# Six instead of four of a unit's 64 blocks of exponentials on VectorE and GpSimd

## The chip, the cores and the metric

The kernel runs on one core of one Trainium2 chip. The metric is device microseconds of that core for one execution, the median of several runs. TensorE multiplies matrices into PSUM, ScalarE (ACT) evaluates exp and tanh, VectorE (DVE) does elementwise work and moves results out of PSUM, GpSimd (POOL) does a little elementwise work, and SyncE (SP) issues most DMAs.

## The reference

```python
def _A_ref(x, wqkv, wo):                        # x 1 x 2048 x 512, H = 32 heads of Dh = 16
    qkv = ((x @ wqkv).reshape(B, S, 3, H, Dh)).transpose(2, 0, 3, 1, 4)
    q, k, v = qkv[0], qkv[1], qkv[2]
    scores = jnp.einsum("bhqd,bhkd->bhqk", q, k) * (Dh ** -0.5)
    p = softmax(scores, axis=-1)
    o = jnp.einsum("bhqk,bhkd->bhqd", p, v)
    return o.transpose(0, 2, 1, 3).reshape(B, S, D) @ wo

def _B_ref(x, w1, w2, w3, w4):
    h = gelu(layernorm(x) @ w1)
    # the four quarters of h's columns shifted by 1, -1, 2, -2 positions
    x1 = x + shifted(h) @ w2
    return x1 + gelu(layernorm(x1) @ w3) @ w4

g = sigmoid((x * gate_w).sum(-1, keepdims=True))
out = g * _A_ref(x, ...) + (1 - g) * _B_ref(x, ...)
```

Attention holds 32 x 2048 x 2048 exponentials. All else is small beside them for ScalarE.

## The kernel before

**Units and blocks.** The queries are cut into four chunks of 512 columns, the 32 heads into eight groups of four. A *unit* (c, u) is one chunk with one group of heads: 32 units. A unit has 16 key tiles of 128 (kt) times four heads (j) = 64 *blocks*. A block is 128 keys by 512 queries of one head: one score matmul with 32 rows of the array (`score`, L620), an exponential of 512 columns, and one matmul with v (`attend_block`, L720) that adds into the unit's accumulator `acc`. There is one accumulator bank (pool `psA`). Column 0 of v is one, so that row of `acc` is the softmax's denominator. At a unit's end `finish_unit` copies `acc` to SBUF (L755), sends the denominators through DRAM to spread them over partitions, and scales (L768, L774).

**Slots.** The program is written out by hand as a row of slots, not scheduled by a tool. In slot i the loop at the end emits ScalarE's exponential of slot i (`expo(i)`, L712: one instruction over two or three blocks), the scores of slot i + 2 (`scores(i + 2)`), the attends that have become ready (`attend_ready`), then work beside the attention (`beside`), filling matmuls with zeros (`fill`, L863), and the steps that have fallen due (`run_due`). The first 34 slots (`EARLY`, the young phase) hold two blocks each; later ones three, in three PSUM banks. Slots alternate between two sides of PSUM, so TensorE writes the scores of a slot while ScalarE reads the one before.

**Blocks that ScalarE doesn't get.** From the third unit on (`DUNIT = 2`) the four blocks of the last key tile (`DKT`, kt = 15) go another way. Four slots of a unit, 1, 4, 7 and 10 after its start (`DAT`), hold two blocks of the row for ScalarE, and the third bank (`dsc`) holds the scores of such a block. `whole` then computes the exponential as a product of a power of two and a cubic polynomial:

- VectorE evacuates the scores times a factor to a 32-bit integer y (L628): the high half is the whole part of the power of two, the low half its fraction.
- GpSimd makes two linear terms of the low half, `ec` (L643) and `ea` (L645), in f16.
- VectorE makes the power of two from the high half, `t0` (`power`, L651, once for each block), then for two blocks at once, 1024 columns: the square of `ec` (L654), plus one (L658), times `ea` (L662), and times the power (`product`, L667), read as bf16.

Two such blocks are a *pair*; two pairs may be open (`epool`, `state["pairs"]`). A finished pair is put in `products`, and `attend_whole` attends it once its unit has an accumulator.

**What sets the order.** `due(slots, rank, cost, fn)` puts a step off by so many slots. `run_due` runs what is due in order of rank, and passes over a step with a cost while the planner's clock says that VectorE is more than `HORIZON` = 1.9 us ahead of TensorE, for at most `OVER` = 4 slots. The clock (`clock`, `vec`, `tensor`, `evac`) is a sum of fixed costs kept while the program is written. `beside` gets a credit for each slot, `CREDIT` = 0.52 us of matmuls, times `DSHARE` = 0.55 in a slot with a block for VectorE, and spends it on projections, the MLP (`gelu_pair`, with tanh on ScalarE, L332, and scalar_tensor_tensor on VectorE, L336), and output tiles (`out_tile`, L446, L454). One matmul of these costs 0.225. `fill` pads TensorE to `FILL` = 2 matmuls a slot, `DFILL` = 1 in a slot with a block for VectorE. `hurry` forces all due steps when a pair's buffers or the accumulator are needed. The q tile of a group of heads is projected from the first slot of the unit before on (`urgent`).

Of the kernel before, what the change touches and what calls it, by code (L numbers as in the profile page):

```python
# [30 lines left out]
def kernel(  # L31
# [51 lines left out]
    otp = ctx.enter_context(tc.tile_pool(name="otp", bufs=2))  # L83
# [71 lines left out]
    state = {"slot": 0, "gen": 0, "young": True, "now": 0, "hurried": 0, "gelus": 0, "mm": 0, "idle": False}  # L155
    later = []
    asides = deque()
    DKT = (NT - 1,)
    DUNIT = 2
    FIRST, CHAIN, TAIL = 0, 1, 2  # L160
    SLACK = 0.3
# [144 lines left out]
    def gelu_pair(w, m, rhs, dst, key):  # L306

        yield from wait_for(lambda: state["gelus"] < 3)
        state["gelus"] += 1
        yh = gelp.tile([P, 2, CH], BF16, tag="yh", name="yh")  # L310
        sq = gelp.tile([P, 2, CH], BF16, tag="sq", name="sq")
        for r in range(2):
            ps = gen("ps_y")
            yield from proj(ps, w, slice((m + r) * P, (m + r + 1) * P), rhs, GELU)
            evac(0.69).tensor_scalar(out=yh[:, r, :], in0=ps[:], scalar1=0.5, scalar2=None, op0=ALU.mult)  # L315
            if r == 0:
                yield MM * GELU
# [12 lines left out]
        def tanh():  # L330
            clock["act"] += 0.97
            nc.scalar.activation(out=sq[:], in_=sq[:], func=ACT.Tanh)  # L332
            due(2, TAIL, 1.2, gate_up)

        def gate_up():
            vec(1.25).scalar_tensor_tensor(out=dst, in0=sq[:], scalar=1.0, in1=yh[:], op0=ALU.add, op1=ALU.mult)  # L336
# [208 lines left out]
    def run_due(all=False):  # L545

        now = state["slot"]
        for item in sorted((x for x in later if x[0] <= now), key=lambda x: (x[1], x[0], x[2])):
# [5 lines left out]
        if asides and now >= EARLY // 2 and max(clock["vector"], clock["act"]) + 0.7 < clock["pe"] + HORIZON:  # L554
# [9 lines left out]
    row, start, todo = [], {}, {}  # L564
    for n, (c, u) in enumerate(units):
        start[n] = len(row)
        todo[(c, u)] = NT if n < DUNIT else NT + len(DKT)
        row += [(c, u, kt, j) for kt in range(NT) if n < DUNIT or kt not in DKT for j in range(4)]

    DAT = (1, 4, 7, 10)  # L570
    slots, extra, i = [], {}, 0
    unit, wait = 0, []
    while i < len(row):
        if i >= start.get(unit + 1, len(row)):
            unit += 1
        if i >= start[unit] and wait is not None and unit >= DUNIT and unit not in extra:
            extra[unit] = True
            wait = [(len(slots) + d, kt, j) for kt in DKT for d, j in zip(DAT, range(4))]
            left = {kt: [0, 1, 2, 3] for kt in DKT}
        w = 2 if len(slots) < EARLY else 3  # L580
        bl = row[i:i + w]
        if wait and len(slots) >= wait[0][0] and i + 2 < len(row):
            kt = wait[0][1]
            free = [j for j in left[kt] if j not in {b[3] for b in row[i:i + 2]}]
            if free and row[i + 1][:2] == units[unit]:
                wait.pop(0)
                left[kt].remove(free[0])
                bl = row[i:i + 2]
                extra[(len(slots),)] = units[unit] + (kt, free[0])
        slots.append((i, bl))  # L590
        i += len(bl)
    assert not wait
    extra = {k[0]: v for k, v in extra.items() if isinstance(k, tuple)}
# [30 lines left out]
    def whole(dsc, c, u, kt, j):  # L624


        y = ypool.tile([P, CH], I32, tag="y", name="y")
        vec(0.69, clock["pe"] + 0.2).tensor_scalar(out=y[:], in0=dsc[:], scalar1=65536.0 * DH ** -0.5 / LN2,  # L628
                                scalar2=127.5 * 65536.0, op0=ALU.mult, op1=ALU.add)
        group = halves.setdefault((c, u, kt), [])  # L630
        r = len(group) % 2
        group.append(j)
        if r == 0:
            while state["pairs"] == 2:
                hurry()
            state["pairs"] += 1
            halves["now"] = [epool.tile([P, 2, CH], t, tag=tag, name=tag)
                             for tag, t in (("t0", I16), ("ea", F16), ("ec", F16))]
        t0, ea, ec = halves["now"]
        lo = y[:].bitcast(U16).rearrange("p (n k) -> p n k", k=2)[:, :, 0]  # L640
        hi = y[:].bitcast(I16).rearrange("p (n k) -> p n k", k=2)[:, :, 1]
        g = LN2 / 65536.0
        nc.gpsimd.tensor_scalar(out=ec[:, r, :], in0=lo, scalar1=g / IM, scalar2=(RE - LN2 / 2) / IM,  # L643
                                op0=ALU.mult, op1=ALU.add)
        nc.gpsimd.tensor_scalar(out=ea[:, r, :], in0=lo, scalar1=CUB * IM * IM * g,  # L645
                                scalar2=CUB * IM * IM * (REAL - LN2 / 2), op0=ALU.mult, op1=ALU.add)

        pair = group[-2:]

        def power():  # L650
            vec(0.44).tensor_scalar(out=t0[:, r, :], in0=hi, scalar1=0.0, scalar2=128.0, op0=ALU.max, op1=ALU.mult)  # L651
# [5 lines left out]
        def one():  # L657
            vec(0.5).tensor_scalar(out=ec[:], in0=ec[:], scalar1=1.0, scalar2=None, op0=ALU.add)  # L658
            due(1, CHAIN, 0.7, cubic)

        def cubic():
            vec(0.75).tensor_tensor(out=ec[:], in0=ec[:], in1=ea[:], op=ALU.mult)  # L662
            due(1, CHAIN, 0.7, product)

        def product():
            pe = t0[:].bitcast(BF16)
            vec(0.75).tensor_tensor(out=pe, in0=ec[:], in1=pe, op=ALU.mult)  # L667
# [56 lines left out]
    def attend(a):  # L724

        c, u, kt, _ = row[a]
# [106 lines left out]
    def attend_ready():  # L833
        while waiting:
            a = waiting[0]
# [3 lines left out]
            if kt == 0 and (accs or state["slot"] < freed["at"] + 2):  # L839
                if not accs or slot_of[a][0] > state["now"] - 3:  # L840
# [4 lines left out]
                continue  # L845
# [19 lines left out]
    for i in range(NS):  # L865
# [4 lines left out]
        while 4 * ready + 3 <= lo + len(bl) - 1:  # L870
            waiting.append(4 * ready)
# [40 lines left out]
```

## Time and profile before

| | |
|---|---|
| median of 3 runs | 954.34 us (952.54 to 955.73) |
| the profiled execution's own time | 954.31 us |
| its span, first to last instruction | 952.1 us |
| mean granted TensorE clock | 0.967 |
| PE busy | 831.2 us (87%) |
| ACT busy | 910.0 us (96%) |
| DVE busy | 625.7 us (66%) |
| POOL busy | 192.8 us (20%) |

Busy time is the union of an engine's instructions. Consecutive matmuls and consecutive activations overlap, so their mean durations don't add up to it. An idle time is put down to the instruction that ended it. In the groups, `out<-in` names tiles, then come the shapes, the count, and after the bar the busy time in us, the mean of one in ns, the idle time in front in us, and what ended it.

### The profile page before, as it was taken

To read this page: it belongs to the slowest core of one execution; us is meant where nothing else is said; L and a number is where in the kernel's file an instruction comes from. 1 tells how busy PE (TensorE), PEld (TensorE's weight loads), DVE (VectorE), ACT (ScalarE), POOL (GpSimd) and SP (SyncE) were. 2 spreads that over 40 slices of the span, in tenths; PEclk is the share of its full clock that TensorE was granted. 3 is DMA by queue.
4 is the path that set the end of the run, shared out by engine and by line. 5 is a ranking of instruction groups with operands and counts; after the bars stand their busy time and mean duration, and the time that the engine had idled before them with its cause. 6 is when DMAs were issued, how large, how long until landed. Compare 5 with 4: busy or idle time off the path is not lost.

```text
span 952.1 us, 14507 instructions
## 1 busy us (share of the span) xinstructions
PE 831.2 (87%) x5631; PEld 252.0 (26%) x5631; DVE 625.7 (66%) x1100; ACT 910.0 (96%) x735; POOL 192.8 (20%) x281
## 2 busy tenths in 40 slices
PE   8999888889988889988789888889888899888886
PEld 2222222222222222222222222222222222222221
DVE  3776788778777764768754877755777744344436
ACT  5889999999999999999999999999999999999994
POOL 3012122222211211212121213112112112222220
PEclk9997999999998999999999989999999999999998
DMA  9601000000000000000000000000000100000000
GB/s 213 191 12 56 1 13 12 12 13 13 1 12 13 12 12 10 26 12 12 13 13 5 9 12 23 24 9 5 12 13 13 34 12 3 12 12 12 13 12 23
DMA packets 30381, 22.28 MB, mean 23 GB/s; under 512 B 16744, under 2 KB 25832, under 8 KB 30312
## 3 DMA queue, kind: packets, MB, share of 16 engines
q1 hardware_dynamic: 28680, 20.17, 7.3%
q10 hardware_dynamic: 1632, 1.18, 0.5%
q8 instruction: 44, 0.72, 0.3%
q14 instruction: 25, 0.20, 0.1%
HBM read 17.17 MB, written 2.35 MB: 21 GB/s over the span
## 4 chain that ended last, share of the span: by engine, by line
ACT 58%; issue 23%; PE 15%; DMA 2%; DVE 2%; SPq 0%; DVEq 0%; ACTq 0%
ACT pt L712 55%; PE stage L620 5%; ACT sq L332 3%; PE acc L720 3%; PE ps_v L209 2%; DMA bcs<-rec_d 1%; PE acc L863 1%; PE ps_y L209 1%; PE ps_o L209 1%; PE ps L209 1%; PE ps_k L209 1%; DMA wq<-in_A_wqkv_dram 1%; PE ps_t L297 0%; PE ps_q L209 0%; DVE rr L792 0%
## 5 line engine op out<-in xcount | busy, mean ns | idle before, releaser
L712 ACT ACTIVATE pt<-stage 128x1536 bf16<-128x1536 f32 (+1 forms) x694 | 882.9, 1492 | 24.1 <-PE stage L620 19.4
L620 PE MATMUL stage<-qT,kT 32*128 32x512 bf16 x1928 | 277.6, 390 | 106.5 <-ACT pt L712 83.8
L643 POOL TENSOR_SCALAR ec<-y 128x512 f16<-128x512 uint16 x120 | 86.0, 717 | 643.0 <-DVE y L628 642.8
L620 PEld LDWEIGHTS <-kT 32*128 32x128 bf16 x2048 | 101.5, 91 | 373.6 <-issue 333.8
L720 PE MATMUL acc<-pt,vp 128*17 128x512 bf16 (+1 forms) x1928 | 194.7, 394 | 0.2
L863 PE MATMUL acc<-wq,zero 128*128 128x512 bf16 x480 | 165.7, 394 | 0.0
L628 DVE TENSOR_SCALAR y<-dsc 128x512 int32<-128x512 f32 x120 | 82.5, 687 | 119.3 <-PE dsc L620 118.8
L209 PE MATMUL ps_y<-xnT,w 128*128 128x512 bf16 x288 | 99.8, 395 | 2.0 <-DVE yh L315 1.4
L645 POOL TENSOR_SCALAR ea<-y 128x512 f16<-128x512 uint16 x120 | 89.0, 742 | 9.5
L315 DVE TENSOR_SCALAR yh<-ps_y 128x512 bf16<-128x512 f32 x72 | 49.6, 689 | 50.2 <-PE ps_y L209 49.7
L720 PEld LDWEIGHTS <-vp 128*17 128x17 bf16 (+1 forms) x2048 | 48.7, 88 | 117.1 <-issue 117.0
L209 PE MATMUL ps<-w,g2T 128*128 128x512 bf16 x224 | 65.9, 384 | 0.0
L651 DVE TENSOR_SCALAR t<-y 128x512 int16<-128x512 int16 x120 | 59.8, 499 | 0.3
L620 PE MATMUL dsc<-qT,kT 32*128 32x512 bf16 x120 | 48.1, 401 | 0.0
L863 PEld LDWEIGHTS <-zero 128*128 128x128 bf16 x480 | 35.6, 98 | 45.0 <-issue 44.8
L654 DVE TENSOR_TENSOR ec<-ec 128x1024 f16<-128x1024 f16 x60 | 41.0, 683 | 4.6 <-POOL ec L643 4.6
L332 ACT ACTIVATE sq<-sq 128x1024 bf16<-128x1024 bf16 x36 | 43.5, 1209 | 0.0
L667 DVE TENSOR_TENSOR t<-ec,t 128x1024 bf16<-128x1024 f16 x60 | 42.6, 710 | 1.3
L662 DVE TENSOR_TENSOR ec<-ec,ea 128x1024 f16<-128x1024 f16 x60 | 41.5, 692 | 2.3
L209 PEld LDWEIGHTS <-w 128*128 128x128 bf16 x288 | 22.8, 97 | 56.1 <-issue 54.2
L774 DVE TENSOR_TENSOR oT<-accsb,bcs 128x512 bf16<-128x512 f32 x31 | 22.4, 724 | 22.5 <-DMA bcs<-rec_d 22.5
L336 DVE SCALAR_TENSOR_TENSOR g2T<-sq,yh 128x1024 bf16<-128x1024 bf16 x28 | 35.3, 1260 | 0.3 <-ACT sq L332 0.3
(81 smaller groups left out, 539.2 us busy)
## 6 DMA issues: line engine op xcount, KB each, us to landing
bcs<-rec_d SPq DMA_DIRECT2D x31, 256.0 KB
w<-in_B_w_dram SPq DMA_DIRECT2D x2, 1792.0 KB
x_sb<-in_A_x_dram SPq DMA_DIRECT2D x14, 128.0 KB
out_dram<-ot SPq DMA_DIRECT2D x14, 128.0 KB
w<-in_B_w_dram SPq DMA_DIRECT2D x2, 512.0 KB
wkv<-in_A_wqkv_dram ACTq DMA_DIRECT2D x1, 512.0 KB
wo_pad<-in_A_wo_dram SPq DMA_DIRECT2D x8, 64.0 KB
den<-accsb SPq DMA_DIRECT2D x31, 8.0 KB
```

What stands on the lines that cost most here:

```text
L209: nc.tensor.matmul(*args, **kwargs)
L315: evac(0.69).tensor_scalar(out=yh[:, r, :], in0=ps[:], scalar1=0.5, scalar2=None, op0=ALU.mult)
L332: nc.scalar.activation(out=sq[:], in_=sq[:], func=ACT.Tanh)
L620: nc.tensor.matmul(out, lhsT=kT[G][32 * j:32 * j + 32, cc, o:o + P], rhs=qTs[(c, G)][32 * j:32 * j + 32, a, :], start=True, stop=True, til ...
L628: vec(0.69, clock["pe"] + 0.2).tensor_scalar(out=y[:], in0=dsc[:], scalar1=65536.0 * DH ** -0.5 / LN2, scalar2=127.5 * 65536.0, op0=ALU.mu ...
L643: nc.gpsimd.tensor_scalar(out=ec[:, r, :], in0=lo, scalar1=g / IM, scalar2=(RE - LN2 / 2) / IM, op0=ALU.mult, op1=ALU.add)
L645: nc.gpsimd.tensor_scalar(out=ea[:, r, :], in0=lo, scalar1=CUB * IM * IM * g, scalar2=CUB * IM * IM * (REAL - LN2 / 2), op0=ALU.mult, op1= ...
L651: vec(0.44).tensor_scalar(out=t0[:, r, :], in0=hi, scalar1=0.0, scalar2=128.0, op0=ALU.max, op1=ALU.mult)
L667: vec(0.75).tensor_tensor(out=pe, in0=ec[:], in1=pe, op=ALU.mult)
L712: nc.scalar.activation(out=pt[:, 0:w], in_=stages.pop(k)[:, 0:w], func=ACT.Exp, scale=DH ** -0.5)
L720: nc.tensor.matmul(accs[(c, u)][32 * j:32 * j + M, :], lhsT=lhsT, rhs=p, start=(kt == 0), stop=(kt == NT - 1), skip_group_check=True, tile ...
L863: nc.tensor.matmul(acc[:], lhsT=zero[:], rhs=wq[:, 0, :], start=False, stop=False, skip_group_check=True)
```

## The change

The blocks (kt, j) = (15, 3), (15, 2), (15, 1), (15, 0), (14, 3), (14, 2) of each unit from the third on go to VectorE and GpSimd, six instead of four. They are placed by position in the row: the first is scored once the row has reached 24 blocks ahead of the unit's start (`DFROM`), the next ones 9 blocks further each (`DSTEP`). A unit's row has 58 blocks. Attends of the row go by key tile as before, of two blocks for kt = 14 and none for kt = 15.

In `whole` the maximum is taken as the scores are evacuated. The power of two is no longer a tile of its own: after the cubic, which is written as bf16, one scalar_tensor_tensor on the bits adds 128 times the high half of y to them as 16-bit integers. y and the bits are then kept for a pair: y in two buffers, `ec` in three of its own pool, `ea` in two, and three pairs may be open, of which two with a chain that hasn't ended. The output tiles' pool has one buffer in place of two.

`due` takes an engine's name: the step is put off by a slot at a time until that engine's clock has passed VectorE's clock at the time of the call by 0.1 us. It is used for a tanh (ScalarE's clock) and for a finished pair (TensorE's clock). `hurry` forces only steps of a chain and finished pairs.

```diff
+    ecpool = ctx.enter_context(tc.tile_pool(name="ecpool", bufs=3))
+    otp = ctx.enter_context(tc.tile_pool(name="otp", bufs=1))
...
-    DKT = (NT - 1,)
+    DBLOCKS = 6
+    DFROM = -24
+    DSTEP = 9
...
-    def due(slots, rank, cost, fn):
+    def due(slots, rank, cost, fn, ready=None):
+        if ready:
+            step, then = fn, clock["vector"]
+            def fn():
+                if clock[ready] < then + 0.1 and not state["force"]:
+                    later.append((state["slot"] + 1, rank, len(made_steps), cost, fn))
+                else:
+                    step()
...
-            due(3, FIRST, 0.0, tanh)
+            due(2, FIRST, 0.0, tanh, "act")
...
+        mine = [] if n < DUNIT else [divmod(4 * NT - 1 - m, 4) for m in range(DBLOCKS)]
+        todo[(c, u)] = len(mine) // 2
+        wanted += [(start[n] + DFROM + DSTEP * m, c, u) for m in range(len(mine))]
+        for kt in range(NT):
+            heads = [j for j in range(4) if (kt, j) not in mine]
+            if heads:
+                groups.append(list(range(len(row), len(row) + len(heads))))
+                row += [(c, u, kt, j) for j in heads]
+                todo[(c, u)] += 1
...
+        if w == 3 and wanted and wanted[0][0] <= i and i + 2 < len(row):
+            unit = wanted[0][1:3]
+            mine = [b for b in stock[unit] if b[1] not in {x[3] for x in row[i:i + 2]}]
...
-        y = ypool.tile([P, CH], I32, tag="y", name="y")
-        vec(0.69, clock["pe"] + 0.2).tensor_scalar(out=y[:], in0=dsc[:], scalar1=65536.0 * DH ** -0.5 / LN2,
-                                scalar2=127.5 * 65536.0, op0=ALU.mult, op1=ALU.add)
+        vec(0.69, clock["pe"] + 0.2).tensor_scalar(out=y[:, r, :], in0=dsc[:], scalar1=65536.0 * DH ** -0.5 / LN2,
+                                                   scalar2=-126.0 * 65536.0, op0=ALU.mult, op1=ALU.max)
...
-            while state["pairs"] == 2:
+            while state["pairs"] == 3 or state["chains"] == 2:
                 hurry()
...
-        def power():
-            vec(0.44).tensor_scalar(out=t0[:, r, :], in0=hi, scalar1=0.0, scalar2=128.0, op0=ALU.max, op1=ALU.mult)
...
         def cubic():
-            vec(0.75).tensor_tensor(out=ec[:], in0=ec[:], in1=ea[:], op=ALU.mult)
-            due(1, CHAIN, 0.7, product)
-        def product():
-            pe = t0[:].bitcast(BF16)
-            vec(0.75).tensor_tensor(out=pe, in0=ec[:], in1=pe, op=ALU.mult)
-            due(2, FIRST, 0.0, lambda: products.append((c, u, kt, pair, pe)))
-        due(1, FIRST, 0.43, power)
+            vec(0.75).tensor_tensor(out=ec[:].bitcast(BF16), in0=ec[:], in1=ea[:], op=ALU.mult)
+            due(1, CHAIN, 1.23, power)
+        def power():
+            bits = ec[:].bitcast(I16)
+            hi = y[:].bitcast(I16).rearrange("p r (n k) -> p r n k", k=2)[:, :, :, 1]
+            state["chains"] -= 1
+            vec(1.23).scalar_tensor_tensor(out=bits, in0=hi, scalar=128.0, in1=bits, op0=ALU.mult, op1=ALU.add)
+            due(1, LAST, 0.0, lambda: products.append((c, u, pair, ec[:].bitcast(BF16))), "pe")
...
     def hurry():
         state["slot"] += 1
-        run_due(True)
+        run_due(True, (CHAIN, LAST))
```

More of the change, by code (lines that the diff above doesn't have):

```diff
@@ L154 @@
     EARLY = 34
-    state = {"slot": 0, "gen": 0, "young": True, "now": 0, "hurried": 0, "gelus": 0, "mm": 0, "idle": False}
+    state = {"slot": 0, "gen": 0, "young": True, "now": 0, "hurried": 0, "gelus": 0, "mm": 0, "idle": False, "half": 0, "chains": 0, "force": False}
     later = []
     asides = deque()
-    DKT = (NT - 1,)
+    DBLOCKS = 6
+    DFROM = -24
+    DSTEP = 9
     DUNIT = 2
     FIRST, CHAIN, TAIL = 0, 1, 2
+    LAST = 1.5
     SLACK = 0.3
@@ L543, in need, with run_due @@
         assert key in made, key
-    def run_due(all=False):
-        now = state["slot"]
-        for item in sorted((x for x in later if x[0] <= now), key=lambda x: (x[1], x[0], x[2])):
+    def run_due(all=False, only=(FIRST, CHAIN, LAST, TAIL)):
+        now, state["force"] = state["slot"], all
+        for item in sorted((x for x in later if x[0] <= now and x[1] in only), key=lambda x: (x[1], x[0], x[2])):
             _, _, _, cost, fn = item
@@ L553, in run_due @@
             fn()
-        if asides and now >= EARLY // 2 and max(clock["vector"], clock["act"]) + 0.7 < clock["pe"] + HORIZON:
+        if TAIL in only and asides and now >= EARLY // 2 and max(clock["vector"], clock["act"]) + 0.7 < clock["pe"] + HORIZON:
             asides.popleft()()
@@ L563 @@
     units = [(c, u) for c in range(NC_) for u in range(NU)]
-    row, start, todo = [], {}, {}
+    row, start, todo, groups, wanted = [], {}, {}, [], []
     for n, (c, u) in enumerate(units):
         start[n] = len(row)
[L567 to L572, printed above, removed]
-    while i < len(row):
[L574 to L579, printed above, removed]
+        mine = [] if n < DUNIT else [divmod(4 * NT - 1 - m, 4) for m in range(DBLOCKS)]
[7 more added lines that the diff above has]
+                todo[(c, u)] += 1
@@ L580 @@
+    slots, extra, mate, i = [], {}, {}, 0
+    stock = {unit: [divmod(4 * NT - 1 - m, 4) for m in range(DBLOCKS)] for unit in units[DUNIT:]}
+    while i < len(row):
         w = 2 if len(slots) < EARLY else 3
         bl = row[i:i + w]
[L582 to L587, printed above, removed]
+        if w == 3 and wanted and wanted[0][0] <= i and i + 2 < len(row):
+            unit = wanted[0][1:3]
+            mine = [b for b in stock[unit] if b[1] not in {x[3] for x in row[i:i + 2]}]
+            if mine:
+                mine = [b for b in mine if b[1] != mate.get(unit)] or mine
+                stock[unit].remove(mine[0])
+                mate[unit] = mine[0][1] if unit not in mate or mate[unit] is None else None
+                wanted.pop(0)
@@ L588 @@
                 bl = row[i:i + 2]
-                extra[(len(slots),)] = units[unit] + (kt, free[0])
+                extra[len(slots)] = unit + mine[0]
         slots.append((i, bl))
         i += len(bl)
-    assert not wait
-    extra = {k[0]: v for k, v in extra.items() if isinstance(k, tuple)}
+    assert not wanted
     NS = len(slots)
@@ L635, in whole @@
                 hurry()
             state["pairs"] += 1
[L637 to L641, printed above, removed]
+            state["chains"] += 1
+            halves["now"] = (ypool.tile([P, 2, CH], I32, tag="y", name="y"), epool.tile([P, 2, CH], F16, tag="ea", name="ea"),
+                             ecpool.tile([P, 2, CH], F16, tag="ec", name="ec"), [])
@@ L729, in attend @@
         need("v", kt)
-        clock["pe"] = max(clock["pe"], max(exp_at[slot_of[a + j][0]] for j in range(4)))
+        clock["pe"] = max(clock["pe"], max(exp_at[slot_of[b][0]] for b in group))
         tensor("attend")
-        for j in range(4):
-            k, n = slot_of[a + j]
-            attend_block(c, u, kt, j, pts[k][:, n * CH:(n + 1) * CH])
+        for b in group:
+            k, n = slot_of[b]
+            attend_block(*row[b], pts[k][:, n * CH:(n + 1) * CH])
         one_done(c, u)
@@ L839, in attend_ready @@
             if kt == 0 and (accs or state["slot"] < freed["at"] + 2):
-                if not accs or slot_of[a][0] > state["now"] - 3:
+                if slot_of[a][0] > state["now"] - 3:
                     break
@@ L869 @@
         scores(i + 2)
-        while 4 * ready + 3 <= lo + len(bl) - 1:
-            waiting.append(4 * ready)
+        while ready < len(groups) and groups[ready][-1] <= lo + len(bl) - 1:
+            waiting.append(groups[ready])
             ready += 1
```

31 lines of the change are left out of this document (16 added, 15 removed).

## The prediction

> **What bounds the kernel now.** I read the page from the top: busy shares, granted clock, and the chain of work that ended last.
>
> ```profile
> span 952.1 us, 14507 instructions
> PE 831.2 (87%) x5631; PEld 252.0 (26%) x5631; DVE 625.7 (66%) x1100; ACT 910.0 (96%) x735; POOL 192.8 (20%) x281
> PEclk9997999999998999999999989999999999999998
> ACT 58%; issue 23%; PE 15%; DMA 2%; DVE 2%; SPq 0%; DVEq 0%; ACTq 0%
> L712 ACT ACTIVATE pt<-stage 128x1536 bf16<-128x1536 f32 (+1 forms) x694 | 882.9, 1492 | 24.1 <-PE stage L620 19.4
> ```
>
> ScalarE is busy 96% of the span, almost all of it in one line, the exponentials (L712), with 24 us of idle time before them. So the time of the program is the number of exponentials times what each takes, plus a start, a tail and some stalls. The wait list says the same from the other side: TensorE waits for ScalarE, hardly the reverse.
>
> ```profile
> POOL ec L643 <- DVE y L628: 642.8, 118, 14.8
> DVE y L628 <- PE dsc L620: 118.8, 51, 8.8
> PE stage L620 <- ACT pt L712: 83.8, 165, 1.3
> ```
>
> The price of one exponential can't be read from its mean duration: consecutive ones overlap, so 540 times the mean of a wide one would exceed the span. It is read from start to start, in stretches between two tanh without idle time. First the timeline of ScalarE, then its groups by shape in the windows 301.6 to 306.9 and 307.9 to 319.0.
>
> ```profile
> 301.62 5.49 ACT L712 ACTIVATE pt<-stage 128x1536 bf16<-128x1536 f32 x4
> 306.94 1.10 ACT L332 ACTIVATE sq<-sq 128x1024 bf16<-128x1024 bf16 x1
> 307.89 11.39 ACT L712 ACTIVATE pt<-stage 128x1536 bf16<-128x1536 f32 x9
> 319.01 1.21 ACT L332 ACTIVATE sq<-sq 128x1024 bf16<-128x1024 bf16 x1
> 319.95 5.21 ACT L712 ACTIVATE pt<-stage 128x1536 bf16<-128x1536 f32 x4
> ```
>
> ```profile
> L712 ACT ACTIVATE pt<-stage 128x1536 bf16<-128x1536 f32 x4 | 5.5, 1478 | 0.0
> ...
> L712 ACT ACTIVATE pt<-stage 128x1536 bf16<-128x1536 f32 x7 | 9.8, 1541 | 0.0
> L712 ACT ACTIVATE pt<-stage 128x1024 bf16<-128x1024 f32 x2 | 2.3, 1156 | 0.0
> ```
>
> Four wide ones take 306.94 - 301.62 = 5.32 us: 1.330 us each. Seven wide and two narrow take 319.01 - 307.89 = 11.12 us; less 7 x 1.330 that leaves 1.81, so 0.905 us for a narrow one. One block of 512 columns less is worth **0.425 us** of ScalarE. A tanh takes 307.89 - 306.94 = 0.95 us.
>
> How much of the rest is stall, from the same groups between 53 us (the first wide exponential) and 940 us:
>
> ```profile
> L712 ACT ACTIVATE pt<-stage 128x1536 bf16<-128x1536 f32 x540 | 763.5, 1591 | 13.4 <-PE stage L620 11.4 <-PE acc L720 1.3
> L712 ACT ACTIVATE pt<-stage 128x1024 bf16<-128x1024 f32 x120 | 141.2, 1177 | 1.9 <-PE dsc L620 1.8 <-PE acc L720 0.2
> L332 ACT ACTIVATE sq<-sq 128x1024 bf16<-128x1024 bf16 x36 | 43.5, 1209 | 0.0
> ...
> L712 ACT ACTIVATE pt<-stage x694: 1017/1536/1820, 10.0 to 937.7; 128x1536 bf16<-128x1536 f32 x135, 128x1024 bf16<-128x1024 f32 x39
> ```
>
> (The last row is the line's own view: the last exponential starts at 937.7.) 540 x 1.330 + 120 x 0.905 + 36 x 0.95 = 861 us of work, in the 886 us up to the end of the last exponential (about 939): **25 us of stall**, 15.3 of it seen as idle time. Part of that has nothing to do with the narrow slots: it lies where TensorE was granted half its clock.
>
> ```profile
> 60.00:795.00 735.00, 644.77 (x4445) 196.20 (x4442) 522.14 (x911) 724.85 (x582) 150.59 (x208) 0.97 0.05 14
> 795.00:940.00 145.00, 128.07 (x885) 38.87 (x882) 62.56 (x108) 142.26 (x112) 31.75 (x40) 0.99 0.03 11
> 425.50:428.90 3.40, 3.40 (x18) 0.47 (x17) 1.35 (x2) 2.89 (x3) 0.00 (x0) 0.50 0.00 0
> 85.00:95.00 10.00, 10.00 (x59) 2.92 (x57) 4.51 (x11) 8.14 (x7) 2.58 (x4) 0.53 0.39 131
> ```
>
> The columns are the window, its length, busy time of PE, PEld, DVE, ACT and POOL, the granted clock and DMA. At a clock of 0.50 to 0.53 ScalarE lost 0.5 of 3.4 us and 1.9 of 10 us, and TensorE was busy throughout.
>
> **The change, part by part.** *The slots.* Before, the plan has 128 + 30 x 60 = 1928 blocks on ScalarE: 34 young slots of two, 120 slots of two with a block for VectorE beside them, 540 of three. After it has 128 + 30 x 58 = 1868: 34 of two, 180 of two with a block beside, (1868 - 68 - 360) / 3 = 480 of three. So 694 slots in both, and 60 of them go from wide to narrow: 60 x 0.425 = **25.5 us** less of ScalarE, the engine that sets the end. It is all on the path.
>
> *More slots with a block beside.* In such a slot TensorE has 0.905 us instead of 1.330 for the same three score matmuls, and must wait for VectorE to empty the extra bank before the slot after next. The trace bounds its loss: if all 25 us of stall belonged to the 120 such slots they would cost 0.21 us each, and 60 more would cost 12.5 us; if none did, nothing. A gain below nothing is possible too, by a few us, since the first wait of each unit for its last product goes (below). The half-clock windows and the units' ends claim about half of the stall, so I take 0.1 us each, **6 us**, and add 1 us for narrow slots that fall more often into a half-clock window.
>
> *VectorE's and GpSimd's chain.*
>
> ```profile
> L628 DVE TENSOR_SCALAR y<-dsc 128x512 int32<-128x512 f32 x120 | 82.5, 687 | 119.3 <-PE dsc L620 118.8
> L643 POOL TENSOR_SCALAR ec<-y 128x512 f16<-128x512 uint16 x120 | 86.0, 717 | 643.0 <-DVE y L628 642.8
> L645 POOL TENSOR_SCALAR ea<-y 128x512 f16<-128x512 uint16 x120 | 89.0, 742 | 9.5
> L651 DVE TENSOR_SCALAR t<-y 128x512 int16<-128x512 int16 x120 | 59.8, 499 | 0.3
> L654 DVE TENSOR_TENSOR ec<-ec 128x1024 f16<-128x1024 f16 x60 | 41.0, 683 | 4.6 <-POOL ec L643 4.6
> L658 DVE TENSOR_SCALAR ec<-ec 128x1024 f16<-128x1024 f16 x60 | 28.0, 467 | 0.6
> L662 DVE TENSOR_TENSOR ec<-ec,ea 128x1024 f16<-128x1024 f16 x60 | 41.5, 692 | 2.3
> L667 DVE TENSOR_TENSOR t<-ec,t 128x1024 bf16<-128x1024 f16 x60 | 42.6, 710 | 1.3
> L336 DVE SCALAR_TENSOR_TENSOR g2T<-sq,yh 128x1024 bf16<-128x1024 bf16 x28 | 35.3, 1260 | 0.3 <-ACT sq L332 0.3
> L454 DVE SCALAR_TENSOR_TENSOR ot<-dd,g_fin,x_sb 128x512 bf16<-128x512 f32 x12 | 9.7, 811 | 0.4
> L774 DVE TENSOR_TENSOR oT<-accsb,bcs 128x512 bf16<-128x512 f32 x31 | 22.4, 724 | 22.5 <-DMA bcs<-rec_d 22.5
> ```
>
> A pair of blocks costs VectorE 2 x 687 + 2 x 499 + 683 + 467 + 692 + 710 = 4924 ns now. The change drops the two powers (L651) and the product (L667) and adds one fused scalar_tensor_tensor over 1024 columns, int16 in and out. No row has it. Its bounds: 710 ns (the product over the same columns) and twice L454, 1622 ns. I take L336, the same operation at the same width: 1260. The pair is then 2 x 687 + 683 + 467 + 692 + 1260 = 4476 ns. The evacuation of scores (L628) keeps its shape; a maximum for an addition I cost at nothing. In all 90 x 4.476 - 60 x 4.924 = **107 us more VectorE**, 626 to 733. GpSimd gets 60 x (717 + 742) ns = 88 us more, 193 to 280, and has 643 us in which it only waits for L628.
>
> Is this hidden? Up to about 795 us, when the MLP ends, VectorE is busy 522 of 735 us; 50 pairs x 4.92 = 246 of that is the chain, 276 the rest. Afterwards the same stretch holds 75 pairs x 4.48 = 336, in all 612 of some 725: 84%. After 795 us VectorE has over half its time free, and the planner's own clock puts off chain steps and MLP evacuations when VectorE runs ahead of TensorE. So the 107 us lie beside ScalarE's work. If that cover went, each us of lateness at L628 that TensorE's lead of two slots doesn't absorb would be a us of ScalarE.
>
> One rule speaks against my price. The Trainium skill, "Vector Engine (DVE) Microarchitecture Reference", section 7, says that an instruction of this form with two sources in SBUF that are not bf16 runs at half throughput. No row here has such a pair (L336 reads two bf16 tiles). By that rule the pair would cost about 1.2 us more, the sum would have 840 us of VectorE, and the time would be that of the first rival below.
>
> *Scored from 24 blocks ahead.* The first pairs of a unit are worked while the unit before still runs, and wait for the accumulator. The sixth block is scored 21 blocks into its unit of 58, its chain of five steps takes some 8 slots (21 blocks): done at block 42, ahead of the unit's end. Before, the fourth block came 10 slots into a unit of 21, the chain ended near slot 18 to 20. So the wait for the last product at a unit's end shrinks; the rows show few us of it ("PE acc" ended 1.3 us of ScalarE's idle time), and I take 0. The q tile needed early is projected from the first slot of the unit before, 34 blocks (12 slots, some 15 us) ahead of use.
>
> *TensorE.* Per unit 15 groups of four attends and 2 pairs become 14 of four, one of two and 3 pairs: one pass more, 30 in all.
>
> ```profile
> L720 PE MATMUL acc<-pt,vp 128*17 128x512 bf16 (+1 forms) x1928 | 194.7, 394 | 0.2
> ```
>
> 194.7 us for 482 groups is 0.40 us each: 12 us more. The 60 slots also lose about one matmul each, of the MLP or of filling, 60 x 0.22 = 13 us less. This nets to nothing, under the 83.8 us in which TensorE waits for ScalarE. The credit for the MLP falls by 60 x 0.23 = 14 of some 250, so it ends about 5% of its slots later, near the same wall time, with 90 slots to spare.
>
> *Small edits, costed at nothing.*
>
> ```profile
> L470 ACTq DMA_DIRECT2D out_dram<-ot x2: 362/364/366, 948.1 to 949.5; - x2
> ```
>
> One buffer instead of two for output tiles: such tiles are 8 matmuls apart, 1.8 credits at 0.52 a slot or 4.6 us, while the last store of all, issued at 949.5, is over by the end at 952.1.
>
> If that cover went, VectorE would wait a us or so at 12 places. Holding a tanh, or a pair's attends, until the planner's clock says that the data is there: ScalarE's idle time before tanh is 0.0 already, so it can only move MLP work later, into the spare slots. No DMA is added or moved past another on SP's queue; GpSimd's queue gets only more of the same two steps.
>
> **Sum.** The profiled execution took 954.3 us (span 952.1 and 2.2 around it), as the median of the three runs, 954.34. 954.3 - 25.5 + 6 + 1 = 935.8; I say **935**.
>
> **Rivals.**
> 1. *Slower: the fused step takes two passes over its data.* Then it costs 2 x 1.22 to 1.26 us, 1.2 us more than planned, 90 times: 108 us that the planner's clock doesn't know of, with VectorE at 90% of the span. The place is L628 behind it in VectorE's queue. If half of the lateness passes through TensorE's two-slot lead to ScalarE, 935 + 54 = 989 us. It decides from 19 / 108, when 18% gets through. For it: no row with two integer sources. Against it: tensor_tensor with two f32 sources in SBUF shows no such loss (L774, 724 ns for 512 columns). That half-rate is what the skill's rule says; no trace here bears it out yet.
> 2. *No gain: VectorE's queue makes the evacuation late.* At 84% of a first-in, first-out queue, L628 can stand behind a step of 1.2 us. If each of the 180 slots lost 0.2 us, that is 36 us less the 12 (120 x 0.1) they lose today: 935 - 7 + 24 = 952. For it: 69 of 120 evacuations now start without VectorE having idled for them. Against it: ScalarE's idle time put down to the extra bank is 1.8 us in all.
> 3. *All of it.* The narrow slots cost nothing more and the units' ends get smoother: 954.3 - 25.5 - 2 = 927 us.
> 4. *Part of it.* TensorE at half clock more often, 12.5 us for the new narrow slots: 954.3 - 25.5 + 12.5 + 3 = 944 us.
>
> **How the numbers follow.** Forecast (930 to 940): 0.49. All of it: 0.21. Part of it: 0.14. No gain: 0.08. Slower: 0.08. The range must leave out no more than 0.2: from 926, the full gain with smoother ends, to 949, part of it with its unknown. The forecast's own range is 930 to 940. Differences under 0.3% (2.9 us) can't be told from no change. Faster 0.84, the same 0.08, slower 0.08.
>
> **What would show it.** Right: 480 wide and 214 narrow exponentials, still 1.33 and 0.905 us from start to start; ScalarE's share of the span still 95% or more; the fused step near 1.25 us x90; VectorE near 79%; GpSimd near 30%. Wrong: a fused step of 2 us or more; ScalarE's idle time above 45 us, ended by the extra bank or by VectorE; MLP evacuations that run on to the last units, so that output tiles pile up at the end.

## The result, and the profile after

The changed kernel takes **928.3 us** (median of 4 runs, 926.9 to 935.1) against 955.0: a ratio of 0.974, 95% interval 0.969 to 0.979. Twelve further runs are told below; a second comparison of the same two kernels gave 0.975 (0.972 to 0.977). The time lies in the stated range, at its lower end; it is nearer to rival 3 (927) than to the forecast (935).

The page of the changed kernel; its profiled execution took 926.85 us:

```profile
span 925.1 us, 14505 instructions
PE 796.2 (86%) x5478; PEld 245.1 (26%) x5581; DVE 754.1 (82%) x1160; ACT 884.4 (96%) x735; POOL 313.0 (34%) x401
PEclk9998999999999999999999999999999999999998
ACT 45%; issue 19%; PE 16%; DVE 15%; DMA 4%; ACTq 0%; DVEq 0%; SPq 0%
```

ScalarE is still busy 96% of the span, and its busy time fell by 910.0 - 884.4 = 25.6 us. VectorE went from 66 to 82%, GpSimd from 20 to 34%. VectorE's share of the chain that ended last rose from 2 to 15%: VectorE now stands more often on the path that sets the end.

ScalarE's groups by shape from its first wide exponential to its last, and the line's own view:

```profile
L723 ACT ACTIVATE pt<-stage 128x1536 bf16<-128x1536 f32 x480 | 687.4, 1545 | 12.5 <-PE stage L634 11.6
L723 ACT ACTIVATE pt<-stage 128x1024 bf16<-128x1024 f32 x180 | 204.1, 1134 | 0.9 <-PE dsc L634 0.5
L345 ACT ACTIVATE sq<-sq 128x1024 bf16<-128x1024 bf16 x36 | 41.6, 1155 | 1.5 <-DVE sq L340 1.5
...
L723 ACT ACTIVATE pt<-stage x694: 1004/1472/1808, 10.2 to 910.7; 128x1536 bf16<-128x1536 f32 x123, 128x1024 bf16<-128x1024 f32 x51
```

480 wide and 180 + 34 narrow exponentials, as counted ahead. From start to start without idle time between them they still take 1.330 and 0.903 us, and a tanh 0.947 (medians). At the prediction's prices (1.330, 0.905, 0.95 us) that is 835.5 us of work, in the 860 us from 51.7 to the end of the last one at 912.1: **some 25 us of stall, as before**. This profile had a granted clock of 0.982, the one before 0.967. In the second profile of each kernel, told below, the same sum gives 26 us for the changed kernel and 29 for the one before. So the stall didn't grow, and the whole 25.5 us came out.

The waits of the changed kernel that answer to those shown before, with three that were too small to show then; the last line is one of the kernel before:

```profile
POOL ec L657 <- DVE y L652: 504.0, 177, 7.2
...
PE stage L634 <- ACT pt L723: 73.8, 157, 1.4
...
DVE y L652 <- PE dsc L634: 51.0, 44, 3.0
...
PEld L634 <- DVE y L652: 30.8, 51, 1.6
...
ACT pt L723 <- PE stage L634: 18.1, 32, 2.9
...
PE stage L634 <- DVE y L652: 7.9, 15, 1.1
```

```profile
PEld L620 <- DVE y L628: 4.0, 9, 0.8
```

TensorE now waits for VectorE's evacuation of an extra bank (y): 7.9 us at its matmuls, 30.8 us at weight loads ahead of them. It was 0.3 and 4.0 us. Then 51 of 120 evacuations found VectorE idle, now 44 of 180 do. It doesn't show in ScalarE's idle time at the scores (18.1 us, 19.4 before). TensorE's lead of two slots is the likely reason; no run varies it.

VectorE's and GpSimd's chain, and the two windows of the prediction:

```profile
L652 DVE TENSOR_SCALAR y<-dsc 128x512 int32<-128x512 f32 x180 | 123.3, 685 | 52.5 <-PE dsc L634 51.0 <-DVE ec L679 0.5
L679 DVE SCALAR_TENSOR_TENSOR ec<-y,ec 128x1024 int16<-128x1024 int16 x90 | 117.9, 1310 | 1.1
L671 DVE TENSOR_TENSOR ec<-ec,ea 128x1024 bf16<-128x1024 f16 x90 | 67.5, 751 | 3.6
L663 DVE TENSOR_TENSOR ec<-ec 128x1024 f16<-128x1024 f16 x90 | 63.2, 703 | 1.5 <-POOL ec L657 1.5
L667 DVE TENSOR_SCALAR ec<-ec 128x1024 f16<-128x1024 f16 x90 | 45.9, 510 | 0.9
L349 DVE SCALAR_TENSOR_TENSOR g2T<-sq,yh 128x1024 bf16<-128x1024 bf16 x28 | 38.5, 1379 | 0.0
L657 POOL TENSOR_SCALAR ec<-y 128x512 f16<-128x512 uint16 x180 | 145.9, 811 | 504.2 <-DVE y L652 504.0
L659 POOL TENSOR_SCALAR ea<-y 128x512 f16<-128x512 uint16 x180 | 149.1, 828 | 14.3
```

```profile
60.00:795.00 735.00, 634.97 (x4447) 196.62 (x4527) 632.77 (x965) 726.07 (x600) 263.44 (x321) 0.98 0.05 14
795.00:915.00 120.00, 106.43 (x730) 32.03 (x740) 80.23 (x112) 114.50 (x93) 39.06 (x48) 1.00 0.04 12
```

The fused step (L679) takes 1310 ns. The steps that run beside GpSimd's are slower than before on average: the cubic 751 for 692, adding one 510 for 467, GpSimd's two 811 and 828 for 717 and 742. Split by whether a GpSimd step runs beside it, the cubic takes 684 ns alone and 814 beside one, and 46 of 90 are beside one (before: 686 alone, 1 of 60 beside one). Adding one takes 417 alone and 559 beside, the fused step 1216 and 1393. The evacuation from PSUM takes 685 ns alone, and no more in the few cases beside one. These longer steps make VectorE's 754 us out of the 733 forecast.

### The profile page after: what moved, and what is told of

It is laid out like the page before. It is cut to its first block, busy times and chain, and to the rows that moved or that the text cites. A ratio compares the mean times of both kernels' runs of the same rounds, so it can differ in the third digit from the quotient of the medians.

```text
span 925.1 us, 14505 instructions
## 1 busy us (share of the span) xinstructions
PE 796.2 (86%) x5478; PEld 245.1 (26%) x5581; DVE 754.1 (82%) x1160; ACT 884.4 (96%) x735; POOL 313.0 (34%) x401
## 4 chain that ended last, share of the span: by engine, by line
ACT 45%; issue 19%; PE 16%; DVE 15%; DMA 4%; ACTq 0%; DVEq 0%; SPq 0%
ACT pt L723 43%; PE stage L634 5%; PE acc L731 3%; DVE ec L679 2%; DMA bcs<-rec_d 2%; DVE y L652 2%; ACT sq L345 2%; PE ps_k L222 1%; PE ps_v L222 1%; PE acc L874 1%; PE ps_o L222 1%; DMA rec_d<-rec 1%; PE ps L222 1%; DVE ec L671 1%; DVE yh L328 1%
## 5 line engine op out<-in xcount | busy, mean ns | idle before, releaser
L723 ACT ACTIVATE pt<-stage 128x1536 bf16<-128x1536 f32 (+1 forms) x694 | 854.6, 1413 | 20.6 <-PE stage L634 18.1
L657 POOL TENSOR_SCALAR ec<-y 128x512 f16<-128x512 uint16 x180 | 145.9, 811 | 504.2 <-DVE y L652 504.0
L652 DVE TENSOR_SCALAR y<-dsc 128x512 int32<-128x512 f32 x180 | 123.3, 685 | 52.5 <-PE dsc L634 51.0
L659 POOL TENSOR_SCALAR ea<-y 128x512 f16<-128x512 uint16 x180 | 149.1, 828 | 14.3
L874 PE MATMUL acc<-wq,zero 128*128 128x512 bf16 x396 | 137.5, 387 | 4.8 <-issue 4.8
L679 DVE SCALAR_TENSOR_TENSOR ec<-y,ec 128x1024 int16<-128x1024 int16 x90 | 117.9, 1310 | 1.1
L671 DVE TENSOR_TENSOR ec<-ec,ea 128x1024 bf16<-128x1024 f16 x90 | 67.5, 751 | 3.6
L634 PE MATMUL dsc<-qT,kT 32*128 32x512 bf16 x180 | 70.4, 391 | 0.0
L667 DVE TENSOR_SCALAR ec<-ec 128x1024 f16<-128x1024 f16 x90 | 45.9, 510 | 0.9
L349 DVE SCALAR_TENSOR_TENSOR g2T<-sq,yh 128x1024 bf16<-128x1024 bf16 x28 | 38.5, 1379 | 0.0
L731 PE MATMUL acc<-ec,vp 128*17 128x512 bf16 x180 | 35.7, 390 | 2.4 <-DVE ec L679 2.4
L785 DVE TENSOR_TENSOR oT<-accsb,bcs 128x512 bf16<-128x512 f32 x31 | 22.4, 722 | 18.3 <-DMA bcs<-rec_d 18.2
```

Source lines behind the costliest of these rows:

```text
L634: nc.tensor.matmul(out, lhsT=kT[G][32 * j:32 * j + 32, cc, o:o + P], rhs=qTs[(c, G)][32 * j:32 * j + 32, a, :], start=True, stop=True, til ...
L652: vec(0.69, clock["pe"] + 0.2).tensor_scalar(out=y[:, r, :], in0=dsc[:], scalar1=65536.0 * DH ** -0.5 / LN2, scalar2=-126.0 * 65536.0, op0 ...
L659: nc.gpsimd.tensor_scalar(out=ea[:, r, :], in0=lo, scalar1=root * CUB * IM * IM * g, scalar2=root * CUB * IM * IM * (REAL - LN2 / 2), op0= ...
L671: vec(0.75).tensor_tensor(out=ec[:].bitcast(BF16), in0=ec[:], in1=ea[:], op=ALU.mult)
L679: vec(1.23).scalar_tensor_tensor(out=bits, in0=hi, scalar=128.0, in1=bits, op0=ALU.mult, op1=ALU.add)
L723: nc.scalar.activation(out=pt[:, 0:w], in_=stages.pop(k)[:, 0:w], func=ACT.Exp, scale=DH ** -0.5)
```

## The experiments

Two theories ran through them. *Theory 1*: the time is the number and width of ScalarE's exponentials, and everything else is hidden. *Theory 3*: VectorE is at its edge, and what is added to it comes out as time. *Theory 2* was that the new schedule, apart from the moved blocks, has a gain of its own.

| kernel | median us | ratio to before (95%) | VectorE busy us, share of its span | clock of the profile |
|---|---|---|---|---|
| before, again | 954.8 | 1.000 (0.998 to 1.003) | 626, 65% | 0.962 |
| four blocks, new way | 956.1 | 1.002 (1.000 to 1.004) | 616, 65% | 0.967 |
| changed, again | 930.2 | 0.975 (0.972 to 0.977) | 753, 81% | 0.980 |
| fill of two | 931.8 | 0.977 (0.975 to 0.979) | 756, 81% | 0.990 |
| six, not fused | 938.6 | 0.985 (0.982 to 0.987) | 759, 81% | 0.959 |
| no readiness waits | 940.6 | 0.986 (0.982 to 0.989) | 757, 80% | 0.953 |
| first block 14 ahead | 949.2 | 0.994 (0.991 to 0.997) | 754, 80% | 0.970 |
| fused step twice | 1007.4 | 1.057 (1.052 to 1.061) | 868, 86% | 0.938 |
| fused twice, booked | 1019.7 | 1.069 (1.067 to 1.071) | 861, 85% | 0.931 |
| plus one on GpSimd | 1039.5 | 1.091 (1.088 to 1.095) | 730, 70% | 0.910 |
| first block 3 ahead | 1048.7 | 1.099 (1.097 to 1.101) | 758, 72% | 0.911 |
| eight blocks | 1061.0 | 1.111 (1.106 to 1.116) | 867, 82% | 0.903 |

### Where the gain comes from

**Four blocks, new way.** The changed kernel with one number put back:

```diff
-    DBLOCKS = 6
+    DBLOCKS = 4
```

> The changed kernel with four blocks of a unit instead of six: new placement, fused step and readiness waits, but ScalarE's work as before (540 wide, 154 narrow exponentials). Theory 1 (the gain is the 60 narrower exponentials alone): 951 to 957 us, the time of before. Theory 2 (the schedule gives a part of its own): 944 to 949 us, 7 us or so below before. Rival (the fused step and waits cost something that the six blocks hide): 958 or more.

956.1 us: the time of before. The new placement, the fused step and the readiness waits have no gain of their own while four blocks are moved; theory 2 falls. From four to six blocks in the same scheme the time falls by 25.9 us (to the 930.2 of the changed kernel again), and the 60 narrower exponentials were priced at 25.5. ScalarE's rows are those of before in count:

```profile
L723 ACT ACTIVATE pt<-stage 128x1536 bf16<-128x1536 f32 x540 | 756.8, 1534 | 17.5 <-PE stage L634 15.7 <-PE acc L731 1.3
L723 ACT ACTIVATE pt<-stage 128x1024 bf16<-128x1024 f32 x154 | 171.7, 1124 | 7.3 <-PE stage L634 6.4 <-PE ps_v L222 0.6
```

### Why placement matters: the accumulator

**First block 3 ahead of its unit**, the last 42 blocks into it:

```diff
-    DFROM = -24
+    DFROM = -3
```

> The changed kernel with the first block scored 3 blocks ahead of its unit instead of 24, the last 42 blocks into it. Theory 1 (scoring ahead matters only in that the last chain ends before the unit): the chain of the last pair, some 21 blocks, ends near block 63 of 58, so each of 30 units waits for it at its end, 0.3 to 1 us of ScalarE each: 937 to 958 us, with waits ended by the accumulator. Rival (the two slots of lead cover it): 927 to 931 us.

1048.7 us, worse than the expectation's worst. The mechanism is the one named there; its price was several times too low. ScalarE's waits, TensorE's attends, and the timeline at the end of one unit (TensorE, VectorE, ScalarE):

```profile
ACT pt L723 <- PE acc L731: 86.6, 32, 5.6
...
L731 PE MATMUL acc<-pt,vp 128*17 128x512 bf16 (+1 forms) x1868 | 198.8, 415 | 32.2 <-DVE accsb L766 32.2
L731 PE MATMUL acc<-ec,vp 128*17 128x512 bf16 x180 | 38.8, 401 | 17.9 <-DVE ec L679 17.8
```

```profile
501.45 0.39 PE L634 MATMUL stage<-qT,kT 32*128 32x512 bf16 x3 [0.41 <-ACT pt L723]
...
501.53 1.21 DVE L679 SCALAR_TENSOR_TENSOR ec<-y,ec 128x1024 int16<-128x1024 int16 x1
...
502.08 1.17 ACT L723 ACTIVATE pt<-stage 128x1024 bf16<-128x1024 f32 x1
...
502.86 1.41 DVE L247 TENSOR_SCALAR qT<-ps_q,mask 128x512 bf16<-128x512 f32 x2
...
503.31 0.39 PE L634 MATMUL stage<-qT,kT 32*128 32x512 bf16 x3 [0.49 <-ACT pt L723]
...
503.63 0.39 PE L731 MATMUL acc<-ec,vp 128*17 128x512 bf16 x2
504.18 0.68 DVE L663 TENSOR_TENSOR ec<-ec 128x1024 f16<-128x1024 f16 x1
504.78 0.68 DVE L766 COPY accsb<-acc 128x512 f32<-128x512 f32 x1
...
505.52 0.61 PE L731 MATMUL acc<-pt,vp 128*32 128x512 bf16 x8 [1.50 <-DVE accsb L766]
...
505.99 3.71 ACT L723 ACTIVATE pt<-stage 128x1536 bf16<-128x1536 f32 x3 [2.74 <-PE acc L731]
```

The last pair's fused step ends at 502.7, its attends run at 503.63, and only then may the accumulator be copied out; the copy stands in VectorE's queue behind two q evacuations and a square and ends near 505.5. There is one accumulator, so the next unit's first attends wait for that copy, and ScalarE stops for 2.74 us until they run. It doesn't lack scores here. Those of its next slot were issued at 501.45 and those of the slot after at 503.31, right behind its own last exponential. What ends its wait are the attends. By the kernel's text an exponential writes one of four `pt` tiles, and the attends have to read a tile before it is written again. ScalarE's 32 waits for attends cost 86.6 us, and 30 of them end within 3 us of the start of a unit's copy. In all 30 units from the third on, a pair's attends are the last before the copy. In the changed kernel that is so in 2. The granted clock fell to 0.911.

**First block 14 ahead**, with `DFROM = -14`:

> The changed kernel with the first block scored 14 blocks ahead instead of 24, the last 31 blocks into its unit of 58, so the last chain ends near block 52 by the plan. Between 24 ahead (928 us) and 3 ahead (1049 us, where ScalarE waited for the accumulator at every unit's end). Theory 1 (it costs only where the chain ends after its unit): 927 to 935 us. Rival (steps put off by VectorE's load make the chain longer than the plan, so any ahead less than 24 costs in proportion, 121 us for 21 blocks): 975 to 995 us.

949.2 us, between the two expectations. ScalarE waited for attends into the accumulator only four times, and more than in the changed kernel (18.1 us) for scores:

```profile
ACT pt L723 <- PE stage L634: 27.6, 48, 2.9
ACT pt L723 <- PE acc L731: 7.5, 4, 4.4
```

By the plan the last chain ends six blocks ahead of its unit's end. In the trace the last fused step ends a median of 2.0 us ahead of the last attends of the unit's row (six blocks are 2.9 us), in 3 of 30 units behind them. The pair's own attends end 2.1 us after its fused step, and in 22 of 30 units they are the last ahead of the copy. So the plan's "chain of 8 slots" is somewhat too short, and it leaves out the wait until a finished pair is attended. Why ScalarE waits longer for scores here isn't shown. From 24 to 14 ahead costs 19 us (10 blocks), from 14 to 3 another 100 us (11 blocks): not in proportion, but far from free.

### How near VectorE is to its edge

**Fused step twice**, the first of the two into a tile that nobody reads afterwards:

```diff
+            nc.vector.scalar_tensor_tensor(out=ea[:].bitcast(I16), in0=hi, scalar=128.0, in1=bits, op0=ALU.mult, op1=ALU.add)
             vec(1.23).scalar_tensor_tensor(out=bits, in0=hi, scalar=128.0, in1=bits, op0=ALU.mult, op1=ALU.add)
```

> The changed kernel with the fused step issued twice, the first time into the tile ea, which nobody reads after it; the planner's clock doesn't count it. VectorE gets 90 x 1.3 = 118 us more that the plan doesn't know of, 872 of 925 us (94%). This is the first rival of the prediction made real. Theory 1 (VectorE's lateness is absorbed by the planner's margins and the two slots of lead): 928 to 934 us. Rival as it was priced (half of the lateness reaches ScalarE): 980 to 990 us. Between them, the excess over 928 divided by 118 is the share that gets through.

1007.4 us: 79 of the added 118 us came out as time, two thirds. Its waits:

```profile
ACT pt L724 <- PE stage L634: 64.6, 85, 2.9
...
PEld L634 <- DVE y L652: 76.0, 80, 3.2
...
PE stage L634 <- DVE y L652: 34.4, 31, 2.7
```

This is the way that the prediction's first two rivals describe: the evacuation late in VectorE's queue, then TensorE, then ScalarE. It isn't the only one. TensorE also waited 16.0 us for the fused step itself, at the attends of pairs, and ScalarE 9.8 us for attends. Over the whole span VectorE was busy only 86% of the time.

**Fused twice, booked.** The same, with both in the planner's clock (`vec(1.23)` at each, and `due(1, CHAIN, 2.46, power)`):

> The fused step issued twice as in the earlier run (1007 us), but both are booked in the planner's clock, and the chain's step has their double cost. Theory 1 (what hurt was the lateness that the plan didn't know of): the MLP is put off, the pairs wait, and the time falls to 935 to 960 us. Theory 3 (VectorE's total is the bound): 995 to 1010 us, little changed.

1019.7 us, no better: theory 3, and 10 us beyond its range. Telling the planner does not help, since it can only put VectorE's work off. Pairs are attended later: they come last before the copy in 13 of 30 units, against 2 in the run that isn't booked. Yet it isn't there that ScalarE loses (1.3 us for attends). TensorE waits longer for evacuations:

```profile
PEld L634 <- DVE y L652: 125.1, 84, 3.1
...
PE stage L634 <- DVE y L652: 84.8, 58, 2.7
```

Why these come later when the steps are booked isn't shown.

**Eight blocks**, from the fourth unit on (`DBLOCKS = 8`, `DSTEP = 7`, `DUNIT = 3`):

> The changed kernel with eight blocks of a unit from the fourth unit on, 7 blocks apart (six from the third on, 9 apart, before). 52 more exponentials go from wide to narrow, 22 us of ScalarE; VectorE gets 26 pairs x 4.6 = 120 us more, 874 us. Theory 1 (VectorE is still hidden): 906 us. Theory 3 (VectorE becomes the bound, 97% of 906): 920 to 945 us, with ScalarE's idle time ended by VectorE or the extra bank, and ScalarE below 93% of the span.

1061.0 us, beyond the worst expectation. ScalarE had 22 us less to do by the plan and waited for 150 us in these rows:

```profile
ACT pt L723 <- PE stage L634: 103.7, 120, 5.8
ACT pt L723 <- PE acc L731: 33.1, 26, 2.3
ACT pt L723 <- PE dsc L634: 13.3, 29, 1.0
```

Late evacuations (TensorE waited 82.9 us for them at its scores) and late attends come together here. With this chain and these buffers eight doesn't pay; the closer spacing (7 blocks for 9) wasn't tried alone.

**Six, not fused.** The old powers and product, the new placement and waits, from the fifth unit on. y is then kept for a block and the powers for a pair. The main lines of the edit:

```diff
+            vec(0.75).tensor_tensor(out=ec[:], in0=ec[:], in1=ea[:], op=ALU.mult)
+            due(1, CHAIN, 0.7, product)
+        def power():
+            vec(0.44).tensor_scalar(out=t0[:, r, :], in0=hi, scalar1=0.0, scalar2=128.0, op0=ALU.max, op1=ALU.mult)
+        def product():
+            vec(0.75).tensor_tensor(out=pe, in0=ec[:], in1=pe, op=ALU.mult)
+            due(1, LAST, 0.0, lambda: products.append((c, u, pair, pe)), "pe")
```

> Six blocks ahead of the unit as in the changed kernel, but with the old power and product (two int16 powers and a product for a pair) in place of the fused step, and from the fifth unit on instead of the third. The later start alone gives ScalarE 12 blocks back: 928 + 5 = 933 us. VectorE gets 84 x (2 x 0.50 + 0.71 - 1.31) = 33 us more, known to the planner. Theory 1 (booked work is hidden as long as the planner can put the MLP off): 931 to 937 us. Theory 3 (VectorE is at its edge, and two thirds of any addition come out as time, as in the run with the fused step twice): 955 us, that is, the fused step is what makes six blocks pay.

938.6 us. Less the 5 us of its later start that is 933.6, some 3 us over the changed kernel (930.2): 1.6 us beyond theory 1's range and far from theory 3. The old power is dearer than the prediction's row had it (499 ns): it takes 416 ns alone and 739 beside a step of GpSimd, and 119 of 168 are beside one. The product is as it was (710):

```profile
L677 DVE TENSOR_SCALAR t<-y 128x512 int16<-128x512 int16 x168 | 108.3, 645 | 0.1
L682 DVE TENSOR_TENSOR t<-ec,t 128x1024 bf16<-128x1024 f16 x84 | 59.9, 713 | 0.4
```

2 x 645 + 713 = 2003 ns stand against 1310. Fusing is a small part of the result: six blocks pay without it, 1.5% against before.

**Plus one on GpSimd.** VectorE relieved instead of loaded:

```diff
-            vec(0.45).tensor_scalar(out=ec[:], in0=ec[:], scalar1=1.0, scalar2=None, op0=ALU.add)
-            due(1, CHAIN, 0.7, cubic)
+            nc.gpsimd.tensor_scalar(out=ec[:], in0=ec[:], scalar1=1.0, scalar2=None, op0=ALU.add)
+            due(2, CHAIN, 0.7, cubic)
```

> The changed kernel with the step that adds one moved from VectorE to GpSimd, not booked in the planner's clock, and one slot more before the cubic. VectorE loses 90 x 0.51 = 46 us, 708 us left; GpSimd gets 90 x 1.3 to 1.5 = 120 to 135 us. Theory 1 (VectorE is hidden at 754 us and the remaining stall is TensorE's): 925 to 930 us. Theory 3 (VectorE's lateness makes the remaining stall of some 25 us): 912 to 920 us. Rival (GpSimd's longer steps hold up VectorE's and lengthen the chain): 935 or more.

1039.5 us, the rival, and far over it: the step took GpSimd 2.9 us (2.77 with no step of VectorE beside it) where I had worked out 1.3 to 1.5 from its rows of 512 columns.

```profile
L667 POOL TENSOR_SCALAR ec<-ec 128x1024 f16<-128x1024 f16 x90 | 261.9, 2910 | 34.5 <-DVE ec L663 28.9
...
DVE ec L671 <- POOL ec L667: 141.6, 69, 4.3
```

VectorE, a queue in order, stood 141.6 us at the cubic with the evacuations behind it. Being busy 70% is no protection when the queue's head waits. Whether less VectorE work alone would shorten the changed kernel stays open.

### The waits and the clock

**No readiness waits**: tanh three slots, and a finished pair two slots after its last step, whatever the planner's clock says.

```diff
-            due(2, FIRST, 0.0, tanh, "act")
+            due(3, FIRST, 0.0, tanh)
-            due(1, LAST, 0.0, lambda: products.append(...), "pe")
+            due(2, LAST, 0.0, lambda: products.append(...))
```

> The changed kernel without the waits for the planner's clock: tanh three slots and a finished pair two slots after its last step, as before the change. Theory 1 (costed at nothing in the prediction): 926 to 931 us. Rival (at 82% VectorE a fixed delay finds the data late, and TensorE or ScalarE stop in their queues): 935 to 950 us, with more idle time ended by the fused step on TensorE or by VectorE's sq on ScalarE.

940.6 us: the two waits together are worth 10 us. ScalarE's idle time in the profiled run (946.7 us) shows it, at the scores and at tanh:

```profile
ACT pt L723 <- PE stage L634: 31.4, 51, 2.9
ACT sq L345 <- DVE sq L340: 4.9, 6, 1.5
```

against 18.1 and 1.5 in the changed kernel.

**The two kernels again**, for their clocks.

> The kernel before, unchanged, to see the granted clock of each of its runs. Theory 1 (the gain beyond the forecast is luck of the clock): its runs scatter between 950 and 958 us, with clocks between 0.965 and 0.98, the faster ones at the higher clock. Theory 2 (the change also steadies the clock): every run lies at 953 to 956 us with a clock of 0.97 or less, below the 0.977 to 0.982 of three of the four runs of the changed kernel.

> The changed kernel, unchanged, for the relation of its time to the granted clock. Before, 0.962 gave 958.7 us and 0.978 gave 949.7, about 5.6 us for 0.01; of the four runs known of the changed kernel 0.982 gave 926.9 and 0.968 gave 935.1. Theory 1 (the gain beyond 19 us is the clock of those runs alone): the new runs centre on 0.970 as before's do and on 933 to 935 us. Theory 2 (the changed kernel is granted a better clock): they centre on 0.977 or more and 926 to 930 us.

Both of these theories on the clock hold in part. Over 63 executions of before the mean is 954.6 us at a clock of 0.971; over nine of the changed kernel it is 929.8 at 0.976. In both, 0.01 of clock goes with 4 to 5 us. On their fitted lines at 0.971 the changed kernel takes 932.2: a gain of 22.4 us at equal clock, and 2.4 us that go with the higher clock. The clocks of the first four runs had a median of 0.979. Whether the changed kernel earns its clock can't be settled. Low clocks and stalls go together (0.91 to 0.93 on average in the five runs of over 1000 us), and the runs don't say which makes which.

**Fill of two.** The filling beside a narrow slot raised (`DFILL = 2`):

> The changed kernel with two matmuls instead of one as the least beside a slot that has a block for VectorE. TensorE gets up to 180 x 0.22 = 40 us more, in slots of 0.905 us. Theory A (filling keeps the granted clock up, and the time follows the clock): clock 0.985 or more and 922 to 927 us. Theory B (TensorE has no room in a narrow slot): 0.1 us more in each of 180, 945 us. Theory C (neither): 926 to 931 us.

931.8 us at a clock of 0.99. The clock rose as theory A says and the time didn't fall. Either the added matmuls took back what the clock gave, or a higher clock gives nothing here; the run can't tell them apart.

## Why the prediction was right, point by point

- **The slots, 25.5 us.** Right in size and place. ScalarE's busy time fell by 25.6 us, and the kernel with four blocks, all else new, has the time of before. This is the mechanism, and it is shown.
- **More slots with a block beside, 6 + 1 us.** Over-sized, and the main reason for 928 in place of 935. The profiled run shows no more stall than before (some 25 us in both). At equal clock the loss is about 25.5 - 22.4 = 3 us. The rest went with the higher clock of the runs, for which the prediction has no term: that part is luck.
- **The fused step at 1260 ns.** 1310, and 1237 in the kernel with four blocks. L349, the same operation on bf16, took 1379 in the same run; with no GpSimd step beside them the two take 1216 and 1214. So the half throughput that the Trainium skill ("Vector Engine (DVE) Microarchitecture Reference", section 7) states for two sources in SBUF that are not bf16 doesn't appear with these int16 sources; here the measurement decides. Rival 1 in its own form is out. The row that the prediction held against it (L774) was no good evidence: at 724 ns for 512 columns it runs at half the pace, for each column, of the product's 710 for 1024.
- **VectorE 733 us, GpSimd 280.** 754 and 313. What failed is taking durations from a run where the two met less. The steps that meet the other engine's grew by 3 to 13%; the evacuation, which reads PSUM, didn't.
- **Hidden below 84%.** The forecast 612 of some 725 us became 633 of 735 (86%), with part of the MLP still to come at 795 us, and ScalarE's stall didn't grow. But how near the edge is I had wrong: I let half of an unbooked lateness through, and in the run with the fused step twice it was 67%.
- **"The planner puts off the MLP, which ends near the same wall time."** It puts it off, but not so little: the last MLP tile is added at 859 us (792 before), 50 us ahead of the last exponential. Of the 90 slots to spare 40 are left. This comes near the prediction's own sign of being wrong, the MLP running on to the last units. But it cost nothing: from the end of the last exponential to the end of the span it is 13.0 us, 12.9 before.

```profile
L402 DVE TENSOR_TENSOR x_sb<-x_sb,ps x16: 677/686/690, 393.8 to 859.3; 128x512 bf16<-128x512 bf16 x16
```

- **Scored from 24 blocks ahead, costed at 0.** Right as a difference to before, wrong as a reading: it is the condition for the gain. At 14 ahead 19 of the 24 us (by the second comparison) are gone, at 3 ahead the kernel is 10% slower than before. I had worked out that the chain ends in time, and not what each unit pays where it doesn't.
- **Readiness waits, costed at 0.** They are worth 10 us with six blocks. "ScalarE's idle time before tanh is 0.0 already" was read from a VectorE at 66%.
- **One output buffer in place of two** wasn't tried alone.

## What to carry to other kernels

Price a block moved off the bound engine from start to start, not from mean durations. Here it came out nearly whole, as long as the engine that took it kept its deadlines. The deadlines matter more than its busy share: here 82% cost some 3 us of 930. In five other runs 70% to 86% cost 8 to 14% of the time: evacuations came late, a unit's last pair was attended late, or the head of the queue waited. So start such chains early enough that the last one ends well ahead of the buffer that they share, and measure the edge by doubling one step before moving more.

## What the runs showed of the hardware

- GpSimd's tensor_scalar on 1024 columns of f16, in place, took 2910 ns, where 512 columns of 16-bit integers to f16 took 852 to 932 ns in the same run. With no step of VectorE beside them it was 2771 and 620 ns.
- A scalar_tensor_tensor with two int16 sources, one of them every second element, ran at the pace of one with two bf16 sources: 1310 against 1379 ns for 1024 columns in the same run, and 1216 against 1214 with no GpSimd step beside them.
- VectorE's steps with 16-bit sources in SBUF took longer beside a GpSimd step (417 ns alone, 559 beside one, for tensor_scalar; 684 and 814 for tensor_tensor), and GpSimd's too (618 and 824). An evacuation from PSUM took the same either way: 684 and 685 ns in the run with plus one on GpSimd, where 51 of 180 were beside a GpSimd step.
- The granted clock moves from run to run (0.959 to 0.981 over the 63 executions of the unchanged kernel before), and 0.01 of it goes with 4 to 5 us of 955.
